# Shared feed-forward weights stored as one float32 word and split at use, a later conversion, a reordered search and two-byte places in an attention, MoE and SwiGLU kernel

## The chip, the cores and the metric

One core of one Trainium2 chip. The metric is the device time of one execution in microseconds; of several runs the median counts.

## The reference

Three stages follow one another. `x` of the second is the attention's output as 2176 tokens of 512 (4 batches of 544).

```python
# 1: attention, 4 batches, 8 heads, 512 local and 32 global positions, 64 wide
a_l = sm(where(mask, q_l @ k_l.T, -1e9) with q_l @ k_g.T in front)   # window 32
out = concat([sm(q_g @ k_all.T) @ v_all, a_l @ concat([v_g, v_l])])
# 2: mixture of 8 experts; all 2176 x 8 logits in falling order, a token goes to
#    the first expert that still has room (cap = 272); the rest stay 0
logits = x @ w_gate
h = maximum(x[mask] @ w1[e], 0.0)          # 512 -> 1024
out[mask] = h @ w2[e]                      # 1024 -> 512
# 3: one shared SwiGLU layer, 512 -> 1536 -> 512
g = x @ w_gate2; silu = g * (1.0 / (1.0 + exp(-g)))
y = (silu * (x @ w_val)) @ w_out
```

The weights of stage 3 (`moe2_...`) come in float64.

## The kernel before

**Attention** runs in 40 units (4 batches, 2 halves of the heads, 4 blocks of rows and one unit for the global rows). The steps of several units are interleaved by a fixed schedule: while TensorE (PE) makes the scores of one unit, ACT takes the exponent (p, L320 and L393) of another, and DVE normalises a third (xt, L352).

**Conversion** (class Convert) runs beside it. The products are of float32, so each of 36 pieces of float64 weights is read as pairs of int32 (`cv_raw`, 512 KB, a DMA on SP's queue, L110), turned by ACT's Abs (`cv_a`, L116) and three operations of DVE (L123 to L125) into a float32 word, and split by two more (L130, L131) into this word and a remainder, since the feed-forward products take a high and a low part. Both parts are stored in HBM (`wd`, L135; two pieces make one tile of 128 x 2 x 1024). 24 pieces (gate and val) are converted during attention: from unit 3 on, each unit calls `step` 1.45 times, and two steps are one piece. The other 12 (w_out) follow in the feed-forward part, where `convert` pays 0.75 per tick against a cost of 1.6 and 1.4 per step, so one piece in four ticks. Each engine works its instructions off in the order in which they were issued, so an operation of a conversion that waits holds all that is behind it.

**Routing** (class Router) assigns the experts in eight phases, one after the other. A phase finds its expert's threshold in six rounds of a search: DVE compares all logits with 32 thresholds (`cmp`, L677), PE counts in 17 matmuls (L682), DVE reduces (`ge`, L685), takes the maximum (`k`, L688) and makes the next thresholds (`lo`, `T`). Then each chosen token gets a place: DVE makes one-hot rows (`ol`, L735, from `iota` in float32 and `lo` in int32), which are the weights of 17 matmuls (L739) that give the list of tokens, and GpSimd (POOL) gathers their rows (`xg`). In phase 0 POOL makes the other factor (`rh`, L730 and L731), later DVE.

**Feed-forward** (class Ffn) takes two experts at a time. For each of them `moe` (w1, w2), and then for both together the shared layer: g and v in 24 silu pairs (three matmuls per product, L1015 to L1017; silu L1096 on ACT, L1097 on DVE, the cast L1098 on ACT, the remainder L1099 on DVE), then o (L1120 to L1122). Weight tiles follow one list. A w1 or w2 tile is loaded as float32 (`raw`, a ring of 4) and split by an ACT copy and a DVE subtraction (`parts`, L975 and L976) into `wHL` (a ring of 6). A g, v or o tile is loaded from `wd` straight into `wHL` (L978), already split; there are 72 such loads. A tick comes after each half of such a pair. Each tick also moves the background forward: the phases of the router for later experts, and the gather and transposes of tokens (`fetch`), in which the transposes follow the gather by GW = 6 ticks.

## Time and profile before

| | us |
|---|---|
| median of 3 runs | 932.53 (930.74 to 933.59) |
| the profiled execution | 928.77 |
| its span | 927.0 |
| PE busy | 847.3 (91%) |
| DVE busy | 536.4 (58%) |
| ACT busy | 330.6 (36%) |
| POOL busy | 111.8 (12%) |

The profile is of one execution, the span is the time from its first to its last instruction. A busy share is an average over stages with different limits; the stretches of the span are read one by one. Matmuls overlap, so that PE's busy time counts less than the sum of their lengths.

### The profile page before, as it was taken

What the parts mean: (1) busy time and instruction counts of PE and PEld (TensorE: products, weight loads), DVE (VectorE), ACT (ScalarE), POOL (GpSimd) and SP (SyncE); (2) the same over time, 40 slices, a digit from 0 to 9 for tenths busy, and PEclk for the clock granted to TensorE, in tenths of its full rate; (3) what the DMA queues carried; (4) which work ended last, traced back from release to release, by engine and by line L of the source; (5) the groups of instructions that cost most, each with busy time, mean ns of one, the idle gap of its engine ahead of it and who ended that gap; (6) DMA issues with size and microseconds to landing.
All of it is one profiled execution on the core that took longest, in us unless ns stands there. A gap on an engine that the chain in (4) does not pass through costs nothing.

```text
span 927.0 us, 19117 instructions
## 1 busy us (share of the span) xinstructions
PE 847.3 (91%) x7567; PEld 782.8 (84%) x7567; DVE 536.4 (58%) x1523; ACT 330.6 (36%) x751; POOL 111.8 (12%) x186
## 2 busy tenths in 40 slices
PE   5699999935959969999999999999999999999997
PEld 5588878724949959978999998899999889999985
DVE  3499988667869877745967765564323236322300
ACT  4588878503223322213422221243222134222200
POOL 5154322102010000012010100201000020000002
PEclk9899999965968999999999999999999999999999
DMA  7889899305346885754373545365456544744411
GB/s 166 256 228 279 267 278 298 131 13 166 94 153 249 338 307 198 281 200 136 115 286 110 200 181 205 120 201 212 176 183 223 186 138 135 270 149 175 166 60 57
DMA packets 113994, 175.80 MB, mean 190 GB/s; under 512 B 57393, under 2 KB 75057, under 8 KB 104689
## 3 DMA queue, kind: packets, MB, share of 16 engines
q1 hardware_dynamic: 110464, 165.54, 53.0%
q0 software_dynamic: 2896, 8.92, 2.7%
q8 instruction: 59, 0.97, 0.4%
q14 instruction: 31, 0.25, 0.1%
q10 hardware_dynamic: 544, 0.13, 0.1%
HBM read 146.77 MB, written 27.79 MB: 188 GB/s over the span
## 4 chain that ended last, share of the span: by engine, by line
PE 55%; issue 20%; DVE 11%; DMA 8%; ACT 3%; SPq 2%; POOL 1%; POOLq 0%; DVEq 0%; ACTq 0%
PE b L1015 11%; PE b L1017 11%; PE b L1016 11%; PE b L1120 4%; PE b L1121 4%; PE b L1122 4%; DMA wd<-cv_f 2%; DVE wHL L976 2%; PE rbank L682 2%; PE s L309 1%; DMA TA<-v_l 1%; DMA cv_raw<-moe_w_gate 1%; PE tr L329 1%; PE o L340 1%; PE tr L364 1%
## 5 line engine op out<-in xcount | busy, mean ns | idle before, releaser
L1015 PE MATMUL b<-yH,wHL 128*128 128x272 f32 x768 | 225.2, 293 | 1.4 <-DVE dL L1099 1.4
L1017 PE MATMUL b<-yH,wHL 128*128 128x272 f32 x768 | 221.7, 289 | 0.0
L1016 PE MATMUL b<-yL,wHL 128*128 128x272 f32 x768 | 221.0, 288 | 0.0
L1015 PEld LDWEIGHTS b<-yH,wHL 128*128 128x128 f32 x768 | 144.9, 189 | 2.7 <-DVE dL L1099 1.7
L1016 PEld LDWEIGHTS b<-yL,wHL 128*128 128x128 f32 x768 | 145.4, 189 | 0.0
L1017 PEld LDWEIGHTS b<-yH,wHL 128*128 128x128 f32 x768 | 145.0, 189 | 0.0
L1098 ACT CAST dH<-b 128x272 fp32r<-128x272 f32 x96 | 37.1, 387 | 173.4 <-DVE b L1097 173.4
L976 DVE TENSOR_TENSOR wHL<-raw,wHL 128x1024 fp32r<-128x1024 f32 x64 | 77.8, 1221 | 36.1 <-ACT wHL L975 32.0
L1097 DVE TENSOR_TENSOR b<-b,si 128x272 f32<-128x272 f32 x96 | 42.9, 447 | 94.0 <-PE b L1017 94.0
L975 ACT CAST wHL<-raw 128x1024 fp32r<-128x1024 f32 x64 | 66.4, 1044 | 84.4 <-PE b L1122 54.0
L1015 PE MATMUL b<-dH,wHL 128*128 128x272 f32 x256 | 75.9, 297 | 2.2 <-ACT wHL L975 2.2
L1015 PE MATMUL b<-xH,wHL 128*128 128x272 f32 x252 | 76.4, 303 | 1.1 <-ACT wHL L975 0.7
L1120 PE MATMUL b<-wHL,dH 128*128 128x512 f32 x192 | 76.5, 398 | 0.0
L1017 PE MATMUL b<-xH,wHL 128*128 128x272 f32 x252 | 74.7, 297 | 1.7 <-DVE wHL L976 1.7
L1121 PE MATMUL b<-wHL,dL 128*128 128x512 f32 x192 | 75.9, 395 | 0.0
L1122 PE MATMUL b<-wHL,dH 128*128 128x512 f32 x192 | 75.8, 395 | 0.0
L1017 PE MATMUL b<-dH,wHL 128*128 128x272 f32 x256 | 74.5, 291 | 0.8 <-DVE wHL L976 0.8
L1016 PE MATMUL b<-xL,wHL 128*128 128x272 f32 x252 | 74.5, 295 | 0.0
L1016 PE MATMUL b<-dL,wHL 128*128 128x272 f32 x256 | 74.3, 290 | 0.0
L1099 DVE TENSOR_TENSOR dL<-b,dH 128x272 fp32r<-128x272 f32 x96 | 42.4, 442 | 43.6 <-ACT dH L1098 43.6
L1042 ACT ACTIVATE dH<-b 128x272 fp32r<-128x272 f32 x64 | 25.5, 398 | 112.7 <-PE b L1017 103.0
L1096 ACT ACTIVATE si<-b 128x272 f32<-128x272 f32 x96 | 38.3, 398 | 51.4 <-PE b L1017 50.1
(236 smaller groups left out, 1642.9 us busy)
## 6 DMA issues: line engine op xcount, KB each, us to landing
wHL<-wd SPq DMA_DIRECT2D x72, 1024.0 KB, 5.9
raw<-moe_w SPq DMA_DIRECT2D x64, 512.0 KB, 3.7
wd<-cv_f SPq DMA_DIRECT2D x36, 512.0 KB, 6.0
cv_raw<-moe_w_gate SPq DMA_DIRECT2D x12, 512.0 KB, 6.1
cv_raw<-moe_w_val SPq DMA_DIRECT2D x12, 512.0 KB, 4.1
cv_raw<-moe_w_out SPq DMA_DIRECT2D x12, 512.0 KB, 6.3
xd<-xt SPq DMA_DIRECT2D x16, 256.0 KB, 5.3
st<-k_l SPq DMA_DIRECT2D x28, 128.0 KB, 4.9
```

The costliest lines, as they stand in the source:

```text
L975: nc.scalar.copy(w[:, 0], raw)
L976: nc.vector.tensor_tensor(w[:, 1], raw, w[:, 0].bitcast(F32), op=ALU.subtract)
L1015: nc.tensor.matmul(out, wH, xH, start=start, stop=False)
L1016: nc.tensor.matmul(out, wH, xL, start=False, stop=False)
L1017: nc.tensor.matmul(out, wL, xH, start=False, stop=stop)
L1096: nc.scalar.activation(si, a, AF.Silu)
L1097: nc.vector.tensor_tensor(b, b, si, op=ALU.mult)
L1098: nc.scalar.copy(dH[:, f, :], b)
L1099: nc.vector.tensor_tensor(dL[:, f, :], b, dH[:, f, :].bitcast(F32), op=ALU.subtract)
L1120: nc.tensor.matmul(ob[i], dh, H[:, f % 2, :], start=f == 0, stop=False)
L1121: nc.tensor.matmul(ob[i], dl, H[:, f % 2, :], start=False, stop=False)
L1122: nc.tensor.matmul(ob[i], dh, L[:, f % 2, :], start=False, stop=f == 11)
```

## The change

The parts of it are:

- `wd` keeps only the float32 word. A conversion loses `rest` (L130, L131) and stores 256 KB, not 512. A g, v or o tile is loaded like the others into the `raw` ring (512 KB, not 1024) and split by `parts`; `pump` splits at most one tile ahead per call.
- In attention unit 3 issues three loads and nothing else, and the conversions go on from unit 6. A piece of w_out costs 0.6 + 1.2 and not 3.0, so 2.4 ticks; after the first load comes a pause of 4.0; two Abs buffers instead of one.
- In a search round the sum `T` is gone: the comparison adds lo itself. The bound on the other side (m1, k2, cd, hi) stands behind the next comparison.
- `ol` is made from two-byte inputs (`iota2`, `lob`), with the token as the outer and the column as the inner dimension, so that a weight column is read with a step of 18 elements. POOL makes `iota2` once, at the start.
- For experts 2 and up the transposes follow the gather by 12 ticks.

```diff
-CV0 = 3
+CV0, CV1 = 3, 6
...
+NC = 24
...
-        s.g = s.gen(0, 24, LD)
+        s.g = s.gen(0, NC, LD, False)
     def rest_of(s, pool):
...
-        s.use(pool, 2, 1, 2)
+        s.use(pool, 2, 2, 2)
...
-        s.g = s.gen(24, 36, 1)
+        s.g = s.gen(NC, 36, 1, True)
     def word(s, n):
...
-        f = s.f[n] = s.pool.tile([128, 2, 512], I32, name="cv_f", bufs=s.fb)
-        w = f[:, 0]
+        w = s.f[n] = s.pool.tile([128, 512], I32, name="cv_f", bufs=s.fb)
...
-    def rest(s, n):
-        V, f = s.nc.vector, s.f[n]
-        return [lambda: V.tensor_scalar(f[:, 1], f[:, 0], i32(0xFFFFF000), None, op0=ALU.bitwise_and),
-                lambda: V.tensor_tensor(f[:, 1].bitcast(F32R), f[:, 0].bitcast(F32), f[:, 1].bitcast(F32), op=ALU.subtract)]
     def store(s, n):
...
-        s.nc.sync.dma_start(s.wd[n // 2, :, :, 512 * h:512 * h + 512].bitcast(I32), s.f.pop(n))
+        s.nc.sync.dma_start(s.wd[n // 2, :, 512 * h:512 * h + 512].bitcast(I32), s.f.pop(n))
+        s.stored = n
-    def gen(s, N0, N, ld):
-        nop = lambda: None
+    def gen(s, N0, N, ld, late):
...
-        for n in range(N0, N + ld + 3):
+        for n in range(N0, N + ld + 2):
...
             def ahead():
...
-            if ld > 1:
+            if not late:
...
-            a = s.word(m - 1) if ok(m - 1) else [nop] * 3
-            c = s.rest(m - 2) if ok(m - 2) else [nop] * 2
-            for i, ops in enumerate(((c[0], a[0], c[1]), a[1:])):
-                for f in ops:
+            if ok(m - 2):
+                s.store(m - 2)
+            if ok(m - 1):
+                ops = s.word(m - 1)
+                ops[0]()
+                yield 0.6
+                for f in ops[1:]:
...
-                if i == 0 and ok(m - 2):
-                    s.store(m - 2)
-                    s.stored = m - 2
-                if m >= N0 + 1:
-                    yield (1.6, 1.4)[i]
-            if ld == 1:
+                yield 1.2
+            if late:
...
+            if n == N0 + ld - 1:
+                yield 4.0
...
 def attention(tc, ctx, t, cv=None, consts=None, early=None):
...
             if early and n == EN:
...
-            if cv and n >= CV0:
+            if cv and n == CV0:
+                cv.step()
+            if cv and n >= CV1:
...
-        s.hb = t([128, 4, NCH], F32, "hb"); s.h3 = t([128, 3, NCH], F32, "h3"); s.ol = t([128, NCH, 128], BF16, "ol"); s.rid = t([128, NCH, 2], BF16, "rid")
+        s.hb = t([128, 4, NCH], F32, "hb"); s.h3 = t([128, 3, NCH], F32, "h3"); s.ol = t([128, 128, NCH + 1], BF16, "ol"); s.iota2 = t([128, 128, NCH + 1], BF16, "iota2"); s.lob = t([128, NCH + 1], BF16, "lob"); s.rid = t([128, NCH, 2], BF16, "rid")
...
+        e.memset(s.lob, 0.0)
...
+        for x in range(2):
+            e.tensor_copy(s.iota2[:, 64 * x:64 * x + 64], s.iota[:, 64 * x:64 * x + 64, None].to_broadcast([128, 64, NCH + 1]))
+            yield
...
-            T, cmp, ge = s.T[:, 0:KS], s.cmp[:, :, 0:KS], s.ge[:, 0:KS]
+            cmp, ge = s.cmp[:, :, 0:KS], s.ge[:, 0:KS]
...
-            def above(k, old):
+            def bound(k):
+                V.tensor_scalar(s.m1, k1, KS - 1.5, 1e38, op0=ALU.is_ge, op1=ALU.mult)
+                V.tensor_scalar(s.k2, k1, 1.0, None, op0=ALU.add)
                 V.scalar_tensor_tensor(s.cd, s.k2, step(k), old, op0=ALU.mult, op1=ALU.add)
-            def least():
                 V.scalar_tensor_tensor(s.hi, s.cd, s.m1, s.hi, op0=ALU.max, op1=ALU.min)
...
             for k in range(NR):
-                V.tensor_tensor(T, Td[:, k], lo.to_broadcast([128, KS]), op=ALU.add)
...
-                    V.tensor_tensor(cmp[:, c0:c1], s.v[:, c0:c1, None].to_broadcast([128, c1 - c0, KS]),
-                                    T[:, None, :].to_broadcast([128, c1 - c0, KS]), op=ALU.is_ge)
+                    V.scalar_tensor_tensor(cmp[:, c0:c1], Td[:, k, None, :].to_broadcast([128, c1 - c0, KS]), lo,
+                                           s.v[:, c0:c1, None].to_broadcast([128, c1 - c0, KS]), op0=ALU.add, op1=ALU.is_le)
+                if k:
+                    bound(k - 1)
...
-                if k:
-                    above(k - 1, old)
...
-                if k:
-                    least()
...
-                V.tensor_scalar(s.m1, k1, KS - 1.5, 1e38, op0=ALU.is_ge, op1=ALU.mult)
-                V.tensor_scalar(s.k2, k1, 1.0, None, op0=ALU.add)
...
-            above(NR - 1, old)
+            V.tensor_reduce(s.em, s.ew.to_broadcast([128, 32]), axis=AX.X, op=ALU.max, apply_transpose=True)
+            bound(NR - 1)
...
-            least()
-            V.tensor_reduce(s.em, s.ew.to_broadcast([128, 32]), axis=AX.X, op=ALU.max, apply_transpose=True)
...
+        V.tensor_copy(s.lob[:, 0:NCH], s.lo)
...
-        for c0, c1 in ((0, 9), (9, NCH)):
+        for c0, c1 in ((0, 8), (8, NCH + 1)):
...
-            V.tensor_tensor(s.ol[:, c0:c1], s.iota[:, None, :].to_broadcast([128, c1 - c0, 128]), s.lo[:, c0:c1, None].to_broadcast([128, c1 - c0, 128]), op=ALU.is_equal)
+            V.tensor_tensor(s.ol[:, :, c0:c1], s.iota2[:, :, c0:c1], s.lob[:, None, c0:c1].to_broadcast([128, 128, c1 - c0]), op=ALU.is_equal)
         yield TQ, 0.0
...
-            nc.tensor.matmul(q, s.ol[:, c, :], s.rh[:, c].rearrange("p k u -> p (k u)"), start=c == 0, stop=c == NCH - 1)
+            nc.tensor.matmul(q, s.ol[:, :, c], s.rh[:, c].rearrange("p k u -> p (k u)"), start=c == 0, stop=c == NCH - 1)
...
-GW = 6
+GW, GL = 6, 12
...
-            yield GW
+            yield GW if k == 1 else GL
...
     def dma(s, m):
...
-        if k not in s.reg:
+        if kind in ("w1", "w2") and k not in s.reg:
...
-        if kind == "w1":
+        if kind in "gvo":
+            dst, src = raw, s.K.wd[s.half(m) // 2]
+        elif kind == "w1":
...
     def here(s, m):
...
-        return s.known(m) and (kind not in ("w1", "w2") or m in s.raw and s.ticks - s.asked[m] >= LAG and s.done_phase >= k)
+        return m in s.raw and s.ticks - s.asked[m] >= LAG and (kind in "gvo" or s.done_phase >= k)
     def parts(s, m):
...
-        if s.tiles[m][0] in ("w1", "w2"):
-            if m not in s.raw:
-                s.dma(m)
-            raw = s.raw.pop(m)
-            nc.scalar.copy(w[:, 0], raw)
-            nc.vector.tensor_tensor(w[:, 1], raw, w[:, 0].bitcast(F32), op=ALU.subtract)
-        else:
-            nc.sync.dma_start(w.bitcast(F32), s.K.wd[s.half(m) // 2])
+        if m not in s.raw:
+            s.dma(m)
+        raw = s.raw.pop(m)
+        nc.scalar.copy(w[:, 0], raw)
+        nc.vector.tensor_tensor(w[:, 1], raw, w[:, 0].bitcast(F32), op=ALU.subtract)
...
     def pump(s, m, look=None):
...
-        n = 1
-        while s.np < min(m + look + 1, len(s.tiles)) and s.here(s.np):
-            split = s.tiles[s.np][0] in ("w1", "w2")
-            if split and n == 0:
-                break
-            n -= split
+        if s.np < min(m + look + 1, len(s.tiles)) and s.here(s.np):
...
     def load(s):
...
-        while s.nd < min(s.np + RAWS, len(s.tiles)):
-            if s.tiles[s.nd][0] in ("w1", "w2"):
-                if not s.known(s.nd):
-                    break
-                s.dma(s.nd)
+        while s.nd < min(s.np + RAWS, len(s.tiles)) and s.known(s.nd):
+            s.dma(s.nd)
...
-        K.wd = dr.tile([18, 128, 2, 1024], F32, name="wd")
+        K.wd = dr.tile([18, 128, 1024], F32, name="wd")
...
```

ACT's queue in attention, units 3 to 6 (cv_a is the Abs of a conversion, p the exponents, ptb, qT and kT copies of other units). Before:

```order
L116 ACTIVATE cv_a<-cv_raw 128x512 x2
L393 ACTIVATE p<-s,gmx 128x544
L281 ACTIVATE qT_175<-tr 64x8x64 x2
L330 COPY ptb<-tr 128x384 x2
L116 ACTIVATE cv_a<-cv_raw 128x512
L320 ACTIVATE p<-s,mx 128x160 x4
```

With the change:

```order
L387 ACTIVATE p<-s,gmx 128x544
L275 ACTIVATE qT_177<-tr 64x8x64 x2
L324 COPY ptb<-tr 128x384 x2
L314 ACTIVATE p<-s,mx 128x160 x4
L402 COPY ptb<-tr 128x384
L402 COPY ptb<-tr 128x128
L402 COPY ptb<-tr 32x128
L387 ACTIVATE p<-s,gmx 128x544
L285 COPY kT_174<-tr 128x3x128
L286 COPY kT_174<-tr 128x96
L324 COPY ptb<-tr 128x384 x2
L116 ACTIVATE cv_a<-cv_raw 128x512 x2
```

The exponent p<-s,gmx stood behind two Abs and now stands eleven rows ahead of them.

DVE's queue in a search round of phase 0, from the new lower end r_lo on. Before:

```order
L691 SCALAR_TENSOR_TENSOR r_lo_95<-r_k_90,r_Td,r_lo_94 128x1
L692 TENSOR_SCALAR r_m_102<-r_k_90 128x1
L693 TENSOR_SCALAR r_k_96<-r_k_90 128x1
L675 TENSOR_TENSOR r_T<-r_Td,r_lo_95 128x32
L677 TENSOR_TENSOR r_cmp<-r_v,r_T 128x288
L677 TENSOR_TENSOR r_cmp<-r_v,r_T 128x256
L685 TENSOR_SCALAR r_ge,r_ke<-rbank,r_nd 128x32
L670 SCALAR_TENSOR_TENSOR r_cd<-r_k_96,r_Td,r_lo_94 128x1
```

With the change:

```order
L689 SCALAR_TENSOR_TENSOR r_lo_95<-r_k_90,r_Td,r_lo_94 128x1
L677 SCALAR_TENSOR_TENSOR r_cmp<-r_Td,r_lo_95,r_v 128x288
L677 SCALAR_TENSOR_TENSOR r_cmp<-r_Td,r_lo_95,r_v 128x256
L670 TENSOR_SCALAR r_m_102<-r_k_90 128x1
L671 TENSOR_SCALAR r_k_96<-r_k_90 128x1
L672 SCALAR_TENSOR_TENSOR r_cd<-r_k_96,r_Td,r_lo_94 128x1
L673 SCALAR_TENSOR_TENSOR r_hi<-r_cd,r_m_102,r_hi 128x1
L687 TENSOR_SCALAR r_ge,r_ke<-rbank,r_nd 128x32
```

Behind r_lo the comparison r_cmp now comes at once, and the four rows of the other bound stand between it and the reduction r_ge.

DVE's queue among the silu pairs of the first group (b<-b,si and dL are L1097 and L1099). Before:

```order
L1099 TENSOR_TENSOR dL_3046<-b_3016,dH_3045 128x272
L124 SCALAR_TENSOR_TENSOR cv_f<-cv_a,cv_f 128x512
L125 SCALAR_TENSOR_TENSOR cv_f<-cv_raw,cv_f 128x512
L1097 TENSOR_TENSOR b_3012<-b_3012,si 128x272
L1099 TENSOR_TENSOR dL_3022<-b_3012,dH_3021 128x272
L741 COPY r_idxf_134<-rbank 128x3
L742 SCALAR_TENSOR_TENSOR r_idx_142<-rbank,r_idxf_134 128x3
L743 CAST r_idxf_134<-r_idx_142 128x3
L130 TENSOR_SCALAR cv_f<-cv_f 128x512
L123 TENSOR_SCALAR cv_f<-cv_raw 128x512
L131 TENSOR_TENSOR cv_f<-cv_f 128x512
L748 TENSOR_TENSOR r_acc<-r_v_80,r_A 128x17
```

With the change:

```order
L122 TENSOR_SCALAR cv_f<-cv_raw 128x512
L731 TENSOR_TENSOR r_ol<-r_iota_128,r_lob 128x128x10
L123 SCALAR_TENSOR_TENSOR cv_f<-cv_a,cv_f 128x512
L124 SCALAR_TENSOR_TENSOR cv_f<-cv_raw,cv_f 128x512
L1082 TENSOR_TENSOR b_2973<-b_2973,si 128x272
L1084 TENSOR_TENSOR dL_3003<-b_2973,dH_3002 128x272
L972 TENSOR_TENSOR wHL<-raw,wHL 128x1024 x2
L122 TENSOR_SCALAR cv_f<-cv_raw 128x512
L123 SCALAR_TENSOR_TENSOR cv_f<-cv_a,cv_f 128x512
L124 SCALAR_TENSOR_TENSOR cv_f<-cv_raw,cv_f 128x512
L1082 TENSOR_TENSOR b_2969<-b_2969,si 128x272
L1084 TENSOR_TENSOR dL_2979<-b_2969,dH_2978 128x272
```

Where two pairs had one conversion of five rows around them there are now a conversion of three rows with each pair and two splits wHL between.

## Rows read from the trace of the kernel before

**Rows 1.** Table of stretches; columns: stretch, length, busy time of each engine, PEclk, DMA share, GB/s.
```profile
38.00:188.00 150.00, 141.71 (x1922) 119.53 (x1918) 124.66 (x289) 115.14 (x312) 45.38 (x80) 0.99 0.81 246
188.00:222.00 34.00, 8.38 (x136) 6.66 (x136) 26.14 (x123) 2.91 (x4) 6.34 (x5) 0.54 0.32 109
265.00:304.00 39.00, 33.59 (x287) 32.46 (x287) 31.34 (x98) 13.44 (x24) 0.00 (x0) 0.81 0.64 224
304.00:350.00 46.00, 37.01 (x295) 36.32 (x293) 35.10 (x89) 13.01 (x31) 2.76 (x3) 0.94 0.85 315
350.00:392.00 42.00, 42.00 (x411) 41.34 (x411) 31.93 (x116) 10.31 (x28) 1.31 (x1) 0.98 0.65 241
485.00:564.00 79.00, 78.80 (x797) 77.45 (x796) 54.97 (x228) 19.05 (x49) 3.37 (x4) 1.00 0.46 165
564.00:927.00 363.00, 356.50 (x2464) 333.18 (x2462) 123.09 (x239) 96.22 (x193) 24.40 (x35) 1.00 0.47 166
```

**Rows 2.** Waits of PE, 28 to 188: total us, times, longest.
```profile
PE s L385 <- ACT p L393: 7.6, 1, 7.6
```

**Rows 3.** Timeline, 30.3 to 34.9: start, length, engine, operation, idle time before it.
```profile
30.33 0.94 SPq L110 DMA_DIRECT2D cv_raw<-moe_w_gate  x2
...
34.72 0.67 ACT L116 ACTIVATE cv_a<-cv_raw 128x512 f32<-128x512 f32 x1 [7.86 <-DMA cv_raw<-moe_w_gate]
```

**Rows 4.** Groups of the page: busy us, mean ns of one, idle time before.
```profile
L976 DVE TENSOR_TENSOR wHL<-raw,wHL 128x1024 fp32r<-128x1024 f32 x64 | 77.8, 1221 | 36.1 <-ACT wHL L975 32.0
...
L975 ACT CAST wHL<-raw 128x1024 fp32r<-128x1024 f32 x64 | 66.4, 1044 | 84.4 <-PE b L1122 54.0
```

**Rows 5.** Groups of DVE by line, whole span.
```profile
L131 DVE TENSOR_TENSOR cv_f<-cv_f 128x512 fp32r<-128x512 f32 x36 | 25.6, 710 | 0.1
...
L130 DVE TENSOR_SCALAR cv_f<-cv_f 128x512 int32<-128x512 int32 x36 | 16.6, 461 | 0.3
```

**Rows 6.** Timeline of the search, 193.7 to 199.3, DVE.
```profile
193.52 0.25 DVE L685 TENSOR_SCALAR_CACHE_REDUCE r_ge<-rbank,r_nd 128x32 bf16<-128x32 f32 x1 [0.46 <-PE rbank L682]
...
194.06 0.22 DVE L691 SCALAR_TENSOR_TENSOR r_lo<-r_k,r_Td,r_gmin 128x1 f32<-128x1 f32 x1
...
196.84 0.79 DVE L677 TENSOR_TENSOR r_cmp<-r_v,r_T 128x288 bf16<-128x288 f32 x2
...
198.10 0.25 DVE L685 TENSOR_SCALAR_CACHE_REDUCE r_ge<-rbank,r_nd 128x32 bf16<-128x32 f32 x1 [0.46 <-PE rbank L682]
...
199.14 0.46 DVE L677 TENSOR_TENSOR r_cmp<-r_v,r_T 128x288 bf16<-128x288 f32 x1
```

**Rows 7.** Timeline of the places of phase 0, 208.4 to 211.4.
```profile
208.45 2.57 DVE L735 TENSOR_TENSOR r_ol<-r_iota,r_lo 128x1152 bf16<-128x1152 f32 x2
208.69 1.26 POOL L730 TENSOR_TENSOR r_h<-r_hb 128x51 f32<-128x51 f32 x1 [40.94 <-DVE r_hb L728]
...
210.02 1.22 POOL L731 TENSOR_TENSOR r_rh<-r_h,r_rid 128x102 bf16<-128x102 f32 x1
211.30 0.25 PE L739 MATMUL rbank<-r_rh,r_ol 128*128 128x6 bf16 x4 [3.54 <-POOL r_rh L731]
```

**Rows 8.** Weight loads (PEld), groups by line.
```profile
L1015 PEld LDWEIGHTS b<-yH,wHL 128*128 128x128 f32 x768 | 144.9, 189 | 2.7 <-DVE dL L1099 1.7 <-issue 0.9
...
L739 PEld LDWEIGHTS <-r_ol 128*128 128x128 bf16 x136 | 4.1, 97 | 4.6 <-DVE r_ol L735 2.5 <-issue 1.9
```

**Rows 9.** Waits between 188 and 351, all engines.
```profile
ACT cv_a L116 <- DMA cv_raw<-moe_w_out: 10.3, 3, 5.1
...
PE xbank L894 <- DVE xL L897: 6.7, 1, 6.7
...
DVE cv_f L123 <- DMA cv_raw<-moe_w_out: 4.6, 1, 4.6
```

**Rows 10.** DMA issues: engine, count, KB each, median us to landing.
```profile
wHL<-wd SPq DMA_DIRECT2D x72, 1024.0 KB, 5.9
raw<-moe_w SPq DMA_DIRECT2D x64, 512.0 KB, 3.7
...
cv_raw<-moe_w_out SPq DMA_DIRECT2D x12, 512.0 KB, 6.3
```

## The prediction

> **What bounds the kernel now.** I read the table of stretches first [rows 1], cut where attention (188), the gather, the experts and the groups end, then what TensorE waits for, then the rows at the few waits that are long. In the table compare, in one row, PE's busy time with the length of the stretch, and then DVE's. From 485 to 564 PE is busy 78.80 of 79.00 us and from 564 to the end 356.50 of 363: there the time is PE's, and whatever VectorE (DVE) or ScalarE (ACT) is given fits underneath, as long as it stays under the length (DVE 54.97 of 79, 123.09 of 363). Before 350 it is different. From 38 to 188 PE is busy 141.71 of 150, DVE 124.66, ACT 115.14 and the DMA engines 81%: four resources near full. From 188 to 222, the first router phase, PE is busy 8.38 of 34 and waits for a chain on DVE. From 265 to 304 and from 304 to 350 PE loses 39.00 - 33.59 = 5.4 and 46.00 - 37.01 = 9.0 us. So the change can earn its time only before 350, and can lose it anywhere.
>
> **The change, part by part.** The sums are made against the profiled execution (928.77 us; span 927.0, so 1.8 lie around it). It is 3.76 below the median 932.53; that is added back at the end.
>
> 1. *Conversions start later in attention.* The largest single wait of PE in attention is 7.6 us, for the exponent's tile p [rows 2]. The timeline shows its cause [rows 3]: SP issues the first load of moe2 weights at 30.33, and ACT's Abs, queued ahead of that exponent, idles 7.86 us until it lands and starts at 34.72. In the new order that unit issues three loads (five before) and no engine work; the Abs stands eleven listed rows later on ACT, behind that exponent and two further rows of exponents with their copies. Three units later is over 10 us (40 units end by 188), the load took about 4.4 (30.33 to 34.72). Gain 7.6. The list of waits holds nothing else above 2 us. The k and q loads stay on SP behind the cv_raw loads, now three rather than five, so no later.
>
> 2. *One word instead of two in attention.* 24 conversions lose the mask and the subtraction: 24 x (461 + 710 ns) = 28.1 us of DVE [rows 5], and 24 stores shrink by 256 KB, 6.3 MB of the 36.9 MB that 246 GB/s make in 150 us [rows 1]. But PE has only 150 - 141.7 = 8.3 us idle from 38 to 188 [rows 1], and its chains are long. Lower end 0 (PE's own stream is the bound), upper end 8.3, less if the conversions, now spread to the last units, delay the last logits. I take 2.5, nearer the lower end because the busy row is so full. Two added copies on POOL (128x1152 each) stand ahead of kT copies; POOL is busy 45.38 of 150 [rows 1], so 0, at worst some 2 us once. Parts 1 and 2: **-10** (from -5 to -16).
>
> 3. *Search rounds, phase 0.* In a round of before, the comparison starts at 196.84, its counts' reduction at 198.10, and the next comparison at 199.14 [rows 6]: 1.04 us from counts to comparison. Between them stand the reduction, cd, k, hi, lo, m1, k2 and T. The change leaves the reduction, k and lo in that place. The first round shows these almost bare: the reduction at 193.52, lo at 194.06 [rows 6], and what depends on it about 0.22 later: 0.76. So 0.28 per later round and some 0.2 in the first: about -1.4 for five intervals. The four bound operations now run while PE counts. A comparison starts 1.26 us before the reduction behind it (196.84, 198.10); its own 0.79 and two operations that wait for one another, 0.22 each, fill 1.23 of that: just hidden, at worst 0.3 a round, +1.5, which is the upper end. In the phases that run under PE's matmuls PE hardly waits for a round.
>
> 4. *Places in two bytes, phase 0.* The two comparisons that make r_ol take 2.57 us from 208.45; POOL's r_rh, queued behind its difference, ends at 211.24, and the 17 matmuls start at 211.30, released by POOL [rows 7]. So a faster r_ol alone is hidden behind POOL: gain 0. If however POOL's two operations (1.26 and 1.22 us for 51 and 102 elements) are stretched by DVE's, which end about 0.2 before them, up to 1.2 is gained. Added on the path: the cast to lob, 0.1 to 0.2. I take -0.5. What r_ol saves in phases 1 to 7 lies under PE but for the end of phase 1, worth at most 0.4. By the Trainium skill ("VectorE: DVE Perf Modes", section "The perf-mode tier table") tensor_tensor runs at twice the rate once both inputs are two-byte; an estimate by that page is some 1.3 us instead of 2.57 for r_ol, and with POOL as releaser the sum would stay. No row of before shows it, since here one input is four bytes wide. Parts 3 and 4 with the step after phase 0: **-2** (from -3 to +1).
>
> 5. *The strided weight load.* r_ol's columns are now 36 bytes apart. No load of such a kind is in the trace. Contiguous two-byte ones take 97 ns, four-byte ones 189 [rows 8]; 136 of them at 0 to 92 ns more are 0 to 12.5 us. I take 0.5: a load overlaps the matmul before it, and 17 of these run in a row only eight times.
>
> 6. *Split at use.* All 72 shared tiles now need an ACT copy (1044 ns) and a DVE subtraction (1221 ns) [rows 4]; one group of two experts uses 18 tiles, 12 of them in its 24 silu pairs, so +14.7 us of DVE and +12.5 of ACT there. The 12 w_out conversions lose 12 x 1.17 = 14.1 us of DVE [rows 5] between 265 and about 375. From 304 to 392 DVE gains about as much as it loses: its 35.10 + 31.93 = 67 us of 88 [rows 1] stay so. Group 0: about **+0.5** (from -5 to +5). In group 1 there is nothing to lose against: 54.97 + 14.7 = 69.7 of 79, still under PE; with waits for ACT's cast between its two operations of a pair it comes near the limit: 0 (to +3). Groups 2 and 3: the 18 tiles each add 44 us to 123.09 of 363: hidden, 0.
>
> 7. *w_out conversions every 2.4 ticks, not 4.* Before, these cost DVE a wait of 4.6 and ACT 10.3 us in three waits [rows 9]. The first load now gets over five ticks before its use, so the 4.6 should go, some 2 of it for PE; four or so splits of group 0 come into the stretch 265 to 304 and take part of that back. **-2** (from -4 to +2). The wait of PE for xL, 6.7 us [rows 9], the most of what 304 to 350 loses, is a queue of DVE and ACT work in front of a transpose; placing the transposes 12 ticks after the gather, not 6, does not empty that queue, so I leave it.
>
> 8. *DMA.* Shared loads fall from 1024 to 512 KB, 36 MB in all; their landing (5.9 us [rows 10]) is hidden after 350. 0.
>
> Sum: -10 - 2 + 0.5 + 0.5 - 2 = -13 on the profiled 928.8, about 915.5; plus 3.76: **919 us**.
>
> **The rivals.**
> *A: only the stall goes.* PE, ACT and DMA in attention leave no room (PE 141.71 of 150), and later gains and losses cancel. -7.6: 932.5 - 7.6 = 925. For: the busy row. Against: the waits of [rows 9] have causes that the change touches.
> *B, slower: ACT is held by w_out's loads.* The stretch from 485 to 564 holds the 24 pairs of group 1, 79 / 24 = 3.3 us a pair, and a pair has two ticks. So 2.4 ticks are 4.0 us, where a w_out load needs 6.3 in the median to land [rows 10] and the Abs is issued one conversion behind it; four ticks were 6.6. ACT works in order: behind a waiting Abs stand silu, the cast of dH and the copies of the splits, and behind these DVE and PE. At most 12 x (6.3 - 4.0) = 28 us more waiting: 919 + 28 = 947. It decides if the loads still land later than 4.0 us after issue. For: ACT already waits 10.3 us with the longer spacing. Against: DMA gets 512 KB less per tile there, a load of the same size lands in 3.7 at other places [rows 10], and the conversion that waits lets the next load come early.
> *C: strided weights are slow.* The full 12.5 us of part 5 come onto the path: 919 + 12.5 = 931.5, no change. For: nothing in the trace. The Trainium skill ("Advanced Engine Details and Errata", section "SBUF Cachelines") says that reads which meet a new 16-byte line each time pay a penalty, and 36 bytes is past that; by it the loads would sit near the upper end. Against: the loads run ahead of matmuls, and in phases 1 to 7 there are only 17 in a row.
>
> **How the numbers follow.** Forecast 0.62, A 0.18, B 0.12, C 0.08. A change under 0.3% (2.8 us) can't be told from none. The forecast's own range is 908 to 929 (parts 1 and 2 make most of it), A lies in it; C reaches to 932, and a small B (one wait in five) to 934. Left out are the full B and the sum of all lower ends, about 0.18. Faster: nearly all of the forecast and A, a little of C: 0.80; same: 0.07, mostly C; slower: 0.13, B.
>
> **What would show it.** Right: no wait of p near 34; attention's end about 10 us before 188; 2.0 us between comparisons in phase 0; PE without waits after about 340. Wrong: long waits of ACT at cv_a<-cv_raw in 255 to 310, with PE slices under 90% there (B); r_ol's weight loads near 190 ns (C); DVE above 95% in 470 to 560 with PE waiting for wHL or dL (part 6); the attention ending at 181 only (A).

## The result and the profile after

The changed kernel takes **943.41 us** in the median (942.40 to 945.95), the kernel before beside it 931.63: a ratio of 1.013 (1.010 to 1.016). The forecast was 919 with a range to 934, the time lies outside it and on the other side. The profiled execution has a span of 941.7 us, 14.7 more than before.

The table gives the length of each stage in the profiled execution, between the starts of DVE's rows in the timeline: the first reduction r_mm after the last logits, the first r_idxf of phases 0 and 1, and the first and last dL of each group's 24 silu pairs.

| stage | before | after | difference |
|---|---|---|---|
| attention, to r_mm | 189.2 | 173.2 | -16.0 |
| phase 0, to r_idxf | 22.8 | 22.5 | -0.3 |
| gather, expert 0, phase 1 | 43.6 | 43.4 | -0.2 |
| expert 1, to the first pair | 51.3 | 57.0 | +5.7 |
| group 0, 24 pairs | 86.3 | 102.2 | +15.9 |
| o, experts 2 and 3 | 93.3 | 94.2 | +0.9 |
| group 1, 24 pairs | 78.5 | 87.4 | +8.9 |
| all the rest to the last pair | 315.0 | 314.7 | -0.3 |

So attention gave more than was forecast, and expert 1 and the pairs of groups 0 and 1 took it back twice. Groups 2 and 3, with as many splits, lost nothing. The stretches (length, busy time of PE, PEld, DVE, ACT and POOL, PEclk, DMA share, GB/s):

```profile
306.00:393.00 87.00, 78.01 (x692) 76.47 (x691) 66.21 (x203) 22.63 (x58) 4.26 (x4) 0.96 0.75 275
```

That was group 0 before. After, expert 1, group 0 and group 1:

```profile
239.00:296.00 57.00, 43.35 (x367) 40.52 (x366) 48.01 (x132) 24.02 (x38) 2.77 (x3) 0.82 0.63 199
296.00:398.00 102.00, 82.52 (x685) 80.37 (x685) 73.62 (x212) 30.79 (x67) 6.11 (x7) 0.88 0.40 130
492.00:580.00 88.00, 84.00 (x757) 82.07 (x756) 65.32 (x216) 28.29 (x63) 3.35 (x4) 0.96 0.24 77
```

PE is busy 82.52 of 102 us in group 0, where before it was busy 78.01 of 87, and 84.00 of 88 in group 1, where it was 78.80 of 79 [rows 1]. The matmuls of the pairs are the same; PE's busy time is longer while PEclk, a mean of the two levels 1.2 and 2.4 GHz, is 0.88 and 0.96 there and was 0.96 and 1.00. PE is granted the lower level for a while after it has stood still: a wait of 7.46 us ends at 323.83 (below), and from 324 to 328 PEclk is 0.50, from 329 to 333 it is 1.00. A wait thus costs more than its own length. DMA is relieved: 40% and 24% where it was 75% and 46%; DVE is busy 72% and 74%. The waits between 239 and 374 (who waits for whom: total us, times, longest):

```profile
ACT cv_a L116 <- DMA cv_raw<-moe_w_out: 21.6, 5, 5.9
DVE cv_f L122 <- DMA wd<-cv_f: 10.6, 4, 4.9
PE rbank L759 <- DVE r_acc L751: 9.2, 2, 7.5
```

ACT waits 21.6 us for loads of w_out (10.3 before, [rows 9]), and DVE 10.6 for its stores. What that looks like in the queues, in the timeline of group 0 (start, length, engine, operation, idle time before it):

```profile
311.32 2.36 DVE L972 TENSOR_TENSOR wHL<-raw,wHL 128x1024 fp32r<-128x1024 f32 x2 [0.51 <-ACT wHL L971]
...
312.58 1.45 SPq L957 DMA_DIRECT2D raw<-wd  x2
...
314.08 0.42 SPq L110 DMA_DIRECT2D cv_raw<-moe_w_out  x1
...
315.99 1.33 SPq L128 DMA_DIRECT2D wd<-cv_f  x1
...
321.50 0.66 ACT L116 ACTIVATE cv_a<-cv_raw 128x512 f32<-128x512 f32 x1 [5.17 <-DMA cv_raw<-moe_w_out]
...
322.20 0.43 DVE L122 TENSOR_SCALAR cv_f<-cv_raw 128x512 int32<-128x512 int32 x1 [4.94 <-DMA wd<-cv_f]
...
323.83 0.17 PE L759 MATMUL rbank<-r_c,r_onesb 128*128 128x8 bf16 x1 [7.46 <-DVE r_acc L751]
```

SP gets to the load of w_out at 314.08, since ahead of it stood two loads of shared tiles, which start at 312.58, when the first of two splits has freed a buffer. The load lands after 321; ACT waits 5.17 us for it with silu behind it, DVE 4.94 us for the store of an older piece, and PE, which has the router's count in its order, 7.46 us for an r_acc that stands behind that in DVE's queue.

In group 1 the conversions are over. Before, PE's longest wait there was 0.2 us. After (total us, times, longest):

```profile
PE rbank L684 <- DVE r_cmp L677: 3.6, 3, 1.8
PE xbank L890 <- DVE xL L893: 1.3, 2, 1.0
```

PE waits for a comparison of the router and for the low part of transposed tokens (xL), and for no split tile. One of these waits in the timeline:

```profile
551.42 2.35 DVE L972 TENSOR_TENSOR wHL<-raw,wHL 128x1024 fp32r<-128x1024 f32 x2
...
555.73 0.79 DVE L677 SCALAR_TENSOR_TENSOR r_cmp<-r_Td,r_lo,r_v 128x544 bf16<-128x544 f32 x1
...
556.57 0.58 PE L684 MATMUL rbank<-r_cmp,r_ohr 128*128 128x32 bf16 x17 [1.58 <-DVE r_cmp L677]
```

Two splits stand on DVE ahead of the comparison, PE stands still for 1.58 us, and from 557.5 to 560.5 PEclk is 0.50.

Phase 0 got only 0.3 us shorter. One round of the search after, on DVE:

```profile
182.71 0.91 DVE L677 SCALAR_TENSOR_TENSOR r_cmp<-r_Td,r_lo,r_v 128x288 bf16<-128x288 f32 x2
...
183.54 0.15 DVE L670 TENSOR_SCALAR r_m<-r_k 128x1 f32<-128x1 f32 x1
...
184.04 0.22 DVE L673 SCALAR_TENSOR_TENSOR r_hi<-r_cd,r_m,r_hi 128x1 f32<-128x1 f32 x1
184.17 0.25 DVE L687 TENSOR_SCALAR_CACHE_REDUCE r_ge<-rbank,r_nd 128x32 bf16<-128x32 f32 x1
...
184.96 0.91 DVE L677 SCALAR_TENSOR_TENSOR r_cmp<-r_Td,r_lo,r_v 128x288 bf16<-128x288 f32 x2
```

From the reduction (184.17) to the comparison (184.96) it is 0.79 us, near the 0.76 of the prediction. But from the comparison (182.71) to the reduction it is 1.46 and not 1.26 [rows 6]: the two comparisons end 0.91 after their start, not 0.79, and the four operations of the bound end just where the reduction starts, with no idle time before it. A round takes 2.25 us, before 2.30. The places, further on in the same stretch:

```profile
192.69 1.50 DVE L731 TENSOR_TENSOR r_ol<-r_iota,r_lob 128x1024 bf16<-128x1024 bf16 x2
192.92 0.59 POOL L726 TENSOR_TENSOR r_h<-r_hb 128x51 f32<-128x51 f32 x1 [43.41 <-DVE r_hb L724]
...
193.59 0.83 POOL L727 TENSOR_TENSOR r_rh<-r_h,r_rid 128x102 bf16<-128x102 f32 x1
194.47 1.16 PE L735 MATMUL rbank<-r_rh,r_ol 128*128 128x6 bf16 x17 [2.69 <-POOL r_rh L727]
```

r_ol takes 1.50 us, not 2.57, and POOL's two operations 0.59 and 0.83, not 1.26 and 1.22 [rows 7], so POOL had been held by r_ol: before and after, each of the two ends 0.1 to 0.2 us after one of r_ol's two operations (1.35 and 1.23 us long before, 0.68 and 0.83 after). What this gives is half taken back by the 17 matmuls, 1.16 us and 0.6 before: their weight loads with a step of 36 bytes are longer [rows 8]:

```profile
L735 PEld LDWEIGHTS <-r_ol 128*128 128x128 bf16 x136 | 9.2, 162 | 7.3 <-DVE r_ol L731 5.8 <-issue 1.2
```

### The profile page after: what moved, and what is told of

The parts are those of the page before. It is cut to its first block, busy times and chain, and to the rows that moved or that the text cites. A ratio compares the mean times of both kernels' runs of the same rounds, so it can differ in the third digit from the quotient of the medians.

```text
span 941.7 us, 19213 instructions
## 1 busy us (share of the span) xinstructions
PE 858.6 (91%) x7567; PEld 794.8 (84%) x7567; DVE 590.9 (63%) x1489; ACT 394.0 (42%) x823; POOL 107.2 (11%) x189
## 4 chain that ended last, share of the span: by engine, by line
PE 53%; issue 20%; DVE 15%; DMA 4%; ACT 4%; POOL 1%; SPq 1%; POOLq 0%; DVEq 0%; ACTq 0%
PE b L1000 9%; PE b L1002 8%; PE b L1001 8%; PE b L1105 4%; PE b L1106 4%; PE b L1107 4%; DVE wHL L972 3%; PE s L303 3%; DMA wd<-cv_f 3%; DVE r_cmp L677 2%; PE tr L323 2%; PE o L334 2%; PE o L339 1%; PE tr L269 1%; PE tr L358 1%
## 5 line engine op out<-in xcount | busy, mean ns | idle before, releaser
L1000 PE MATMUL b<-yH,wHL 128*128 128x272 f32 x768 | 229.1, 298 | 0.4 <-DVE yL L1050 0.4
L1002 PE MATMUL b<-yH,wHL 128*128 128x272 f32 x768 | 225.2, 293 | 0.0
L1001 PE MATMUL b<-yL,wHL 128*128 128x272 f32 x768 | 224.7, 293 | 0.0
L972 DVE TENSOR_TENSOR wHL<-raw,wHL 128x1024 fp32r<-128x1024 f32 x136 | 163.8, 1222 | 45.0 <-ACT wHL L971 44.9
L971 ACT CAST wHL<-raw 128x1024 fp32r<-128x1024 f32 x136 | 139.2, 1047 | 79.3 <-PE b L1107 52.2
L1000 PEld LDWEIGHTS b<-yH,wHL 128*128 128x128 f32 x768 | 148.7, 194 | 8.5 <-issue 7.7
L1001 PEld LDWEIGHTS b<-yL,wHL 128*128 128x128 f32 x768 | 149.1, 194 | 0.0
L1002 PEld LDWEIGHTS b<-yH,wHL 128*128 128x128 f32 x768 | 148.6, 193 | 0.0
L1000 PE MATMUL b<-xH,wHL 128*128 128x272 f32 x252 | 75.2, 298 | 1.6 <-DVE dL L1028 0.8
L1002 PE MATMUL b<-xH,wHL 128*128 128x272 f32 x252 | 74.0, 294 | 2.2 <-DVE wHL L972 2.2
L872 POOL DMA_INDIRECT xg<-xd,r_idx x24 | 22.8, 949 | 309.5 <-DVE r_idxf L739 123.1
```

What stands on the lines that cost most here:

```text
L971: nc.scalar.copy(w[:, 0], raw)
L972: nc.vector.tensor_tensor(w[:, 1], raw, w[:, 0].bitcast(F32), op=ALU.subtract)
L1000: nc.tensor.matmul(out, wH, xH, start=start, stop=False)
L1001: nc.tensor.matmul(out, wH, xL, start=False, stop=False)
L1002: nc.tensor.matmul(out, wL, xH, start=False, stop=stop)
```

## The experiments

Theory 1: the time is lost in chains of waits that the faster w_out conversions make (load or store late, ACT and DVE held in order). Theory 2: the splits give DVE more to do than it can do beside PE while the router runs, so that PE waits for what DVE does late. Both name the split at use, so parts of the change are taken alone first. The kernel before ran again beside each set of runs (medians of 929.2 to 931.6 us), so the ratios are compared rather than the medians. The stages of all kernels, measured as in the table above (us; "attention" to "expert 1" as there):

| kernel | median | ratio to before | attention | phase 0 | expert 1 | group 0 | group 1 |
|---|---|---|---|---|---|---|---|
| before | 931.6 | | 189.2 | 22.8 | 51.3 | 86.3 | 78.5 |
| the change | 943.4 | 1.013 (1.010 to 1.016) | 173.2 | 22.5 | 57.0 | 102.2 | 87.4 |
| late | 923.2 | 0.993 (0.990 to 0.995) | 184.1 | 23.2 | 50.6 | 85.7 | 78.5 |
| direct | 927.8 | 0.998 (0.997 to 1.000) | 186.4 | 22.8 | 52.1 | 87.5 | 78.7 |
| pace | 937.5 | 1.009 (1.006 to 1.012) | 173.1 | 22.5 | 49.9 | 91.3 | 92.0 |
| queue | 940.1 | 1.011 (1.008 to 1.014) | 174.0 | 22.9 | 53.3 | 97.8 | 85.9 |
| dose | 943.1 | 1.014 (1.012 to 1.016) | 185.1 | 23.2 | 56.5 | 93.0 | 86.5 |
| pool | 956.2 | 1.028 (1.026 to 1.031) | 172.8 | 22.5 | 60.0 | 103.8 | 92.7 |
| writeback | 952.2 | 1.025 (1.023 to 1.027) | 172.7 | 22.5 | 60.8 | 110.8 | 80.0 |
| places | 946.6 | 1.017 (1.014 to 1.020) | 175.1 | 23.2 | 57.3 | 102.6 | 87.7 |
| norest | 916.3 | 0.985 (0.982 to 0.988) | 185.0 | 23.2 | 51.6 | 77.9 | 78.5 |
| mixed | 915.8 | 0.986 (0.983 to 0.990) | 184.9 | 23.2 | 49.9 | 77.5 | 80.8 |
| halfstore | 917.0 | 0.985 (0.983 to 0.988) | 182.7 | 23.2 | 52.2 | 82.2 | 78.5 |
| nohold | 949.1 | 1.021 (1.018 to 1.024) | 173.1 | 22.9 | 52.9 | 104.1 | 90.7 |

Stages that are left out lie within some 3 us of each other. Attention varies by 2.3 us between kernels that are the same up to its end (late, direct, dose and mixed: 184.1 to 186.4).

**late**: the kernel before, with the late start of the conversions alone.

```diff
+            elif n == N0 + ld - 1:
+                yield 4.0
...
-            if cv and n >= CV0:
+            if cv and n == CV0:
+                cv.step()
+            if cv and n >= CV1:
```

> The kernel before with one part of the change alone: attention's conversions start late (three loads in unit 3, the rest from unit 6). If the 7.6 us wait for p was all that this part is worth, 924 us (931.6 - 7.6) and attention ends near 181. If attention has more to give only through the smaller DVE and DMA work of the one-word conversion, the same 924. If the stall merely moves to a later unit, 930 to 932.

923.2 us, 6.0 less than before beside it, and attention 5.1 shorter (2.8 to 5.1 over the four kernels with this attention). The wait for p is gone, the longest of PE in attention is now 2.3 us; the late start is worth less than its 7.6 us.

**direct**: the change without the split at use and without the two-byte places (before's Convert operations, `parts`, `load` and `r_ol`).

> The change without the split at use (both parts stored, shared tiles loaded already split, conversion of five operations and of before's pace) and without the two-byte places. If the split at use is what costs the time behind phase 0, the stages from expert 1 on are as long as in the kernel before and the whole takes 918 to 923 (attention about -8, search -1.5). If the later transposes or the reordered search cost it, group 0 and group 1 stay long and the whole takes over 935.

927.8 us, more than expected, and every stage behind phase 0 within about 1 us of before. So the split at use, with the conversions that belong to it, or the two-byte places (see places) make the loss. Against late, the reordered search and the later transposes cost 4.6 us rather than gain, 2.3 of it in attention, where the two kernels are the same.

**pace**: the change with `yield 1.6` and `yield 1.4` for w_out.

> The change with w_out's conversions at the old pace (1.6 and 1.4 per step, four ticks a piece). Theory 1, ACT and DVE are held by w_out's loads and stores, which come too late for 2.4 ticks: ACT's waits for cv_raw fall from 21.5 us to about 10, group 0's 24 pairs shorten from 102 us by 8 to 12, the whole 931 to 935. Theory 2, DVE has more work than PE in groups 0 and 1 through the splits: work is the same, group 0 within 3 us, the whole 940 to 946. Group 1 (87 us for its pairs, 78.5 before) stays long by both.

937.5 us. ACT's waits for w_out fall to 5.5 us and DVE's for its stores vanish; expert 1 is 7.1 and group 0 10.9 us shorter, as theory 1 has it. But group 1 grows by 4.6, and group 0 stays 5 longer than before. The whole lies between the two expectations, and its interval (1.006 to 1.012) overlaps that of the change: the pace is a part of the loss, not all.

**queue**: the change with w_out's loads and stores on POOL's queue.

```diff
-        s.nc.sync.dma_start(dst, src)
+        (s.nc.gpsimd if nm == "moe2_w_out" else s.nc.sync).dma_start(dst, src)
...
-        s.nc.sync.dma_start(s.wd[n // 2, :, 512 * h:512 * h + 512].bitcast(I32), s.f.pop(n))
+        (s.nc.gpsimd if n >= NC else s.nc.sync).dma_start(s.wd[n // 2, :, 512 * h:512 * h + 512].bitcast(I32), s.f.pop(n))
```

> The change with w_out's loads and stores issued on POOL's queue instead of SP's. Theory 1a, they are late because SP holds them behind loads of shared tiles that wait for a split to free their buffer: ACT's waits for cv_raw and DVE's for wd<-cv_f fall below a third, the whole 927 to 934. Theory 1b, they are late because 2.4 ticks are less than their landing time: the waits stay within a third of 21.5 and 10.6 us, the whole 938 to 945. Theory 2 (DVE's work): 940 to 946.

940.1 us, ACT's waits 10.6 and DVE's 4.3: halved. Between the two expectations: SP's order accounts for about half of the waits. Expert 1 gets 3.7 and group 0 4.4 us shorter; in the whole the intervals (1.008 to 1.014 and 1.010 to 1.016) overlap, so that a gain is not shown.

**dose**: late, and for each shared tile one DVE reduction that serves nothing.

```diff
             nc.sync.dma_start(w.bitcast(F32), s.K.wd[s.half(m) // 2])
+            nc.vector.tensor_reduce(s.dose, s.K.identf[:, None, :].to_broadcast([128, 8, 128]), axis=AX.X, op=ALU.max)
```

> The kernel late (923 us) plus one reduction over 1024 elements on DVE, about 1.2 us, for each of the 72 shared tiles, with no ACT copy, no wait and no DMA changed; it serves nothing. Theory 2, DVE's work alone makes groups 0 and 1 longer: the 24 pairs of group 0 take 92 to 102 us (86 in late) and those of group 1 85 to 90 (78.5), groups 2 and 3 unchanged, the whole 936 to 946. Theory 1, it is the chain from load to ACT to DVE that the split makes: the pairs stay within 3 us and the whole under 930.

943.1 us: 20 more than late, from DVE time alone, without an added ACT copy, a changed transfer or a new wait. Its operation is as long as a split's subtraction [rows 4], and group 1, with the same operations as in late otherwise, takes 86.5 us. The group of the dose in its profile (busy us, mean ns of one):

```profile
L984 DVE TENSOR_REDUCE dose<-identf 128x8 f32<-128x1024 f32 x72 | 87.3, 1213 | 0.9
```

Its stretches of expert 1, group 0 and group 1:

```profile
255.00:307.00 52.00, 42.08 (x364) 39.69 (x365) 44.71 (x125) 17.72 (x29) 0.85 (x1) 0.85 0.63 228
307.00:401.00 94.00, 79.50 (x662) 77.92 (x661) 77.64 (x214) 22.39 (x58) 4.28 (x4) 0.91 0.66 236
493.00:580.00 87.00, 81.42 (x795) 79.50 (x793) 66.42 (x238) 18.45 (x49) 3.37 (x4) 0.98 0.41 148
```

PE's waits in group 1 (total us, times, longest):

```profile
PE rbank L686 <- DVE r_cmp L681: 2.8, 2, 1.4
PE xbank L899 <- DVE xL L902: 2.0, 1, 2.0
```

Expert 1 grows by 5.9, group 0 by 7.3, group 1 by 8.1 us, and groups 2 and 3 by nothing. Theory 2 holds for group 1. In expert 1 and group 0 dose shows that DVE's work can cost time there, not how much the change lost by it, since in dose DVE still has the five operations of a conversion; pace leaves 5 us in group 0 and nothing in expert 1. DVE is busy 66.42 of 87 us in group 1, 76%: on the average it is not full. PE waits, as in the change, at the few places at which its order has a count of the router or a transpose, when DVE reaches the comparison late behind silu and a dose.

**pool**: the change with the subtraction of shared tiles on POOL (`nc.gpsimd.tensor_tensor`).

> The change with the subtraction of the 72 shared tiles on POOL; ACT's copies and the loads stay. Theory 2 (DVE's work): group 1's pairs return from 87 to 78 to 81 us and group 0's from 102 to 88 to 94, the whole 920 to 930. Theory 1 (chain and queues): the chain is as long or longer, the whole 940 or more. If POOL's operation takes over 6 us, PE waits for it and every group gets longer.

956.2 us: theory 2 seemed to fail, but the timeline shows why the test did not take the work off DVE:

```profile
526.12 4.77 POOL L972 TENSOR_TENSOR wHL<-raw,wHL 128x1024 fp32r<-128x1024 f32 x2
...
526.19 0.18 DVE L751 SCALAR_TENSOR_TENSOR r_acc<-rbank,r_Mb 128x17 f32<-128x17 f32 x1
...
526.41 4.52 DVE L752 TENSOR_TENSOR r_A<-r_A,r_acc 128x17 f32<-128x17 f32 x1
```

POOL's two subtractions run 4.77 us from 526.12; a DVE operation over 17 elements, 0.18 us elsewhere, starts at 526.41 and ends with them, after 4.52. The operation just before it, r_acc, which reads rbank from PSUM, took its usual 0.18 beside the same subtractions. DVE was held while POOL worked. pool therefore says nothing against theory 2.

**writeback**: group 0 splits and also stores both parts (on POOL's queue), groups 1 to 3 load them already split.

```diff
+            if s.tiles[m][0] in "gvo":
+                nc.gpsimd.dma_start(s.K.wd2[s.half(m) // 2], w.bitcast(F32))
+        else:
+            nc.sync.dma_start(w.bitcast(F32), s.K.wd2[s.half(m) // 2])
...
```

> The change with the split of shared tiles made once: in group 0 both parts are also stored (on POOL's queue), and groups 1 to 3 load 1 MB per tile already split, as the kernel before did. If group 1 is long because of its 18 splits: its pairs 78 to 80 us, not 87, the whole 931 to 936. If the bandwidth of the 1 MB loads matters behind 400 us, groups 2 and 3 get longer too. Group 0 stays at 100 to 106 us.

952.2 us, not 931 to 936. Group 1 is back at 80.0 us: its loss was its splits. Groups 2 and 3 are no longer. Group 0 is not as expected: 110.8 us, since w_out's loads land later still beside the stores (10.0 us in the median, 6.6 in the change), and the waits of theory 1 grow:

```profile
ACT cv_a L116 <- DMA cv_raw<-moe_w_out: 36.9, 6, 8.9
DVE cv_f L122 <- DMA wd<-cv_f: 24.0, 4, 9.1
```

**places**: the change with before's r_ol.

> The change without the two-byte places: one float32 input, contiguous weight columns. The 17 matmuls of a phase take 0.6 us again, not 1.2 (8 phases, 5 us of PE), and r_ol two times 1.29 us, not 0.75 (8.6 us of DVE in all). If PE's time is what counts from phase 0 on: 938 to 940. If DVE's work does: 945 to 950. Both about equal: 941 to 945.

946.6 us; the intervals of the two ratios (1.014 to 1.020 and 1.010 to 1.016) overlap. About equal, with a lean to DVE's time. The strided loads cost some 0.6 us per phase and are paid by DVE's saving. So the two-byte places are not what made the loss.

**norest**: late with conversions that make no low part (the mask and the subtraction are left out, the word is stored in both places).

```diff
-        return [lambda: V.tensor_scalar(f[:, 1], f[:, 0], i32(0xFFFFF000), None, op0=ALU.bitwise_and),
-                lambda: V.tensor_tensor(f[:, 1].bitcast(F32R), f[:, 0].bitcast(F32), f[:, 1].bitcast(F32), op=ALU.subtract)]
+        return [lambda: None] * 2
...
-        s.nc.sync.dma_start(s.wd[n // 2, :, :, 512 * h:512 * h + 512].bitcast(I32), s.f.pop(n))
+        f = s.f.pop(n)
+        for u in range(2):
+            s.nc.sync.dma_start(s.wd[n // 2, :, u, 512 * h:512 * h + 512].bitcast(I32), f)
```

> The kernel late (923 us) whose conversions make no low part: the mask and the subtraction are left out and the word is stored in both places, so the stored bytes stay and the low parts are wrong. In attention it asks what the one-word conversion earned beyond the late start (attention ended at 184 in late, at 173 in the change). If it was the 28 us of DVE: attention ends at 173 to 176. If it was the 6.3 MB of stores: 182 to 185. Behind phase 0 the 12 conversions of w_out lose 14 us of DVE as well: group 0 shorter by 3 to 6 us if DVE's work counts there. The whole 905 to 912, or 920 to 923.

Attention ends at 185.0, not earlier than in late: 28 us less of DVE bring nothing there. Group 0 is 7.8 us shorter, for 14 us less of DVE: theory 2 again, and more than the 3 to 6 expected.

**mixed**: late with w_out alone kept as one word and split at use, at the old pace.

```diff
-        if s.tiles[m][0] in ("w1", "w2"):
+        if s.tiles[m][0] in ("w1", "w2", "o"):
...
```

> The kernel late with one part of the split at use: w_out alone is kept as one word (stores of 256 KB, loads of 512 KB into the raw ring, ACT copy and DVE subtraction at use), at the old pace; gate and val as before. It takes 14 us of DVE out of the stretch in which the router runs and adds 6 splits to each o stage, where DVE is 40% busy. If DVE's work between 255 and 393 is what counts: group 0 and expert 1 together shorter by 3 to 8 us than in late, o stages as long, the whole 916 to 921. If the chain of loads and splits costs by itself, o stages get longer and the whole is 923 or more.

915.8 us, 0.986 of before: faster than both kernels. Its split at use costs group 1 some 2 us and o nothing; the likely reason is that it falls where the router hardly works. Group 0 has PE nearly full:

```profile
300.00:379.00 79.00, 76.50 (x696) 75.14 (x695) 62.41 (x190) 27.46 (x63) 4.52 (x5) 1.00 0.66 237
```

**halfstore**: late with all five operations, but only the word is stored; the loads take it into both halves of wHL.

```diff
-        s.nc.sync.dma_start(s.wd[n // 2, :, :, 512 * h:512 * h + 512].bitcast(I32), s.f.pop(n))
+        s.nc.sync.dma_start(s.wd[n // 2, :, 512 * h:512 * h + 512].bitcast(I32), s.f.pop(n)[:, 0])
...
-            nc.sync.dma_start(w.bitcast(F32), s.K.wd[s.half(m) // 2])
+            nc.sync.dma_start(w.bitcast(F32), s.K.wd[s.half(m) // 2][:, None, :].to_broadcast([128, 2, 1024]))
```

> The kernel late with all five operations per conversion, but only the word is stored (256 KB, one DMA); a shared tile's load of 1 MB takes the word into both halves, so the low parts are wrong. DVE's work is that of late, the stored bytes are those of the change. If the stores' bytes are what the one-word conversion earned in attention: attention ends at 172 to 176, as in the change, and the whole takes 910 to 914. If it was something else (the 24 larger store issues gone with norest's second DMA, or DVE and DMA only together): 182 to 186 and 921 to 924.

Attention ends at 182.7: the bytes alone bring 1.4 us, which is within the spread of 2.3, as DVE's work alone brought nothing, and both together 11. The row of the stretch from 80 to 140 suggests how. In late:

```profile
80.00:140.00 60.00, 56.10 (x740) 47.68 (x739) 51.19 (x119) 46.67 (x125) 16.63 (x29) 0.97 0.90 263
```

In norest:

```profile
80.00:140.00 60.00, 54.49 (x710) 45.92 (x709) 38.84 (x94) 44.13 (x119) 14.06 (x28) 0.97 0.92 270
```

In halfstore:

```profile
80.00:140.00 60.00, 56.65 (x757) 48.77 (x758) 56.12 (x122) 48.70 (x131) 20.85 (x34) 1.00 0.87 245
```

In the change:

```profile
80.00:140.00 60.00, 59.87 (x835) 51.76 (x833) 45.69 (x110) 51.40 (x139) 19.26 (x37) 1.00 0.90 262
```

In norest DVE falls to 38.84 of 60 us but DMA stays at 0.92 and PE at 54.49; in halfstore DMA falls to 0.87 and 245 GB/s and DVE rises to 56.12, 94%. Only with both is PE at 59.87 of 60. norest also issues two store transfers per piece, so SP's share in it was not told apart; and the kernel with both is the change itself, which also stores a piece ahead of the next one's operations. late with these two alone was not run.

The whole, 917.0 us, lies between the two expectations. Behind phase 0 the smaller stores shorten group 0 by 3.5 us with DVE's work unchanged, so the 8 us of mixed, which stores less of w_out as well, need not be DVE's alone.

**nohold**: pace without the extra tick that holds the router's steps while conversions run.

> The kernel pace (937 us) without the extra tick by which the router's steps are held while conversions run; no work is added or removed. If groups 0 and 1 together are bound by DVE's work, what moves between them is conserved: group 1's pairs shorter than 92 us by as much as group 0's get longer than 91, and the end of group 1 within 4 us of pace's 568.6. If the hold itself costs the time (the router late, PE's order waiting for it): the end of group 1 over 8 us earlier.

949.1 us, and neither expectation came true: group 0 is 12.8 longer than in pace and group 1 only 1.3 shorter. The hold, then, helps. The router's work is not simply moved; in group 0 it meets conversions and splits, and there DVE is busy 80.70 of 104 us with another 10.4 of waiting for ACT's casts:

```profile
293.00:397.00 104.00, 84.47 (x745) 82.61 (x744) 80.70 (x239) 32.45 (x69) 6.55 (x7) 0.90 0.45 135
```

Why group 1 gains so little from having less of the router's work was not tried.

## Why the prediction was wrong

*Parts 1 and 2, attention: -10 forecast, -16 measured, at the end of the range, and right in sign.* The late start gave 3 to 5 us in attention of its 7.6 (late). Part 2 was mis-sized, 2.5 taken and about 11 measured, and its reason was wrong: it weighed DVE's work against PE's idle time alone. The rows fit a DVE and a DMA that were both near their limit (51.19 of 60 us and 0.90 in late), so that norest and halfstore each gave next to nothing and the two together let PE run full; that it was these two and nothing else in the change is not shown. The row with four resources near full was read as "little to gain"; by these runs one of them alone gains little. The upper end of the prediction, 7.6 + 8.3, was reached: PE now runs nearly full from 38 to 171.

```profile
38.00:171.00 133.00, 131.16 (x1806) 112.72 (x1804) 101.15 (x234) 108.65 (x295) 42.99 (x80) 1.00 0.79 231
```

*Parts 3 and 4, phase 0: -2 forecast, -0.3 measured.* The step that failed is "just hidden": it let two of the bound's four operations fill the time (0.44 us), where the four take 0.72 from 183.54 to 184.26; they end only where the reduction starts, 0.2 us later than in the old round, and the merged comparison is 0.12 us longer. What was left on the chain from reduction to comparison (0.79) was right. That POOL was stretched by r_ol was right too, 1.06 us, against 0.6 of slower weight loads. By the Trainium skill ("VectorE: DVE Perf Modes", section "The perf-mode tier table") r_ol should take half the time with both inputs in two bytes (before, both had four); the rows show 2.57 and 1.50, a factor of 1.7 with 2304 elements instead of 2176, so the trace agrees roughly.

*Part 5, strided weights: 0.5 forecast, about 4.5 in PE's time (8 times 0.56).* The bounds held: 162 ns stand between 97 and 189. The step "a load overlaps the matmul before it" failed, since these matmuls stream six columns and do not hide the loads: 17 take 1.16 us, not 0.6. The rule of the Trainium skill in rival C ("Advanced Engine Details and Errata", section "SBUF Cachelines") has the right sign; no run shows that the 16-byte lines are the cause. places shows that DVE's saving pays for it, so C did not decide the time.

*Part 6, the splits: +0.5 in group 0 and 0 in group 1 forecast; +15.9 and +8.9 measured. This is the step that decides.* It compared sums of DVE work with the length of a stage ("still under PE", 69.7 of 79). dose shows that this is no test: with DVE at 76% of group 1 the same work costs 8.1 us, and writeback, without the splits in group 1, has 80.0 there. PE's order has the router's counts and the transposes in it, DVE works silu, splits, conversions and the router in one order, and a burst of two splits (2.4 us) in front of a comparison stops PE (1.58 us at 556.57), whose clock then falls. A wait of 6.7 us of that kind was in [rows 9] and was set aside. "DVE gains about as much as it loses" was also wrong: in group 0 DVE is busy 73.62 us, 66.21 before. And it was wrong in place: the 14 us that the conversions lose were worth 8 us in group 0 (norest), so DVE already set that stretch in part. How much of the 5 us that pace leaves in group 0 is the splits' DVE work is open.

*Part 7 and rival B: -2 forecast for expert 1, +5.7 measured.* The mechanism of rival B was seen, but given 0.12. Its price was 28 us at the most; pace shows 7.1 in expert 1 and 10.9 in group 0, of which group 1 and other stages take some 10 back, so that some 4 (by the ratios) to 8 (by the spans) are left in the whole. Its point of decision was well placed: loads of w_out landed in 6.6 us in the median against 4.0.

```profile
cv_raw<-moe_w_out SPq DMA_DIRECT2D x12, 512.0 KB, 6.6
```

What the forecast missed is that B and the splits' work act in the same stages. Rival B's time, 947, came nearer than the forecast partly by luck: of its mechanism pace shows 4 to 8 us of the whole, and dose, by DVE's work alone, 20.

## What to carry to other kernels

A mean busy share does not say whether an in-order engine can take more work: look for the places at which the bounding engine waits for it, and dose them with an idle operation of the size in question before moving work there. Where two resources are near their limit, relieving one alone may show nothing (norest, halfstore), and relieving both a lot (the change, if it is these two). Work that is moved from a one-time conversion to every use belongs where the receiving engine's other users are quiet, as w_out's split in the o stage, not gate's and val's beside the router.

## What the runs showed of the hardware

- DVE and POOL hold one another. POOL's subtraction over 128x1024 float32 takes 2.47 us, and a DVE operation with two inputs over 17 elements took 4.52 us, and not 0.18, beside two of them; in phase 0 POOL's 51 elements took 1.26 us beside the old r_ol, in places too, and 0.59 beside the new. The Trainium skill ("SBUF — State Buffer", section "Who interferes with whom") says that a DVE instruction with two SBUF inputs contends with a POOL instruction that reads SBUF; the trace agrees.
- A weight load of 128 two-byte columns with a step of 36 bytes takes 162 ns, contiguous 97; matmuls of 6 columns behind such loads follow each other in 68 ns (1.16 us for 17), not 35.
- A wait of PE costs more than itself: in group 0 PE's busy time for the same pairs rises from 78.0 (692 recorded matmuls) to 82.5 us (685) while PEclk falls from 0.96 to 0.88.
